# Attention and mixer on one core: the first 768 columns as one block, its second channel product by seven half-size products, and a third raw-score buffer

## The chip, the cores and the metric

The kernel runs on one core of a Trainium2 chip. The metric is the device time of one execution in microseconds (us). In the profile PE is the tensor engine, PEld its weight loads, DVE the vector engine, ACT the scalar engine, POOL the GpSimd engine and SP the engine that issues most DMAs. PEclk is the granted clock of PE, 1.00 being 2.4 GHz.

## The reference

```python
def _attn_ref(q, k, v, w_pre, w_post):            # (4, 12, 448, 64) each; w: 12 x 12
    scores = scale * np.matmul(q, k.transpose(0, 1, 3, 2))
    scores = np.einsum('bhij,hg->bgij', scores, w_pre)
    scores = scores - np.max(scores, axis=-1, keepdims=True)
    attn = np.exp(scores)
    attn = attn / (np.sum(attn, axis=-1, keepdims=True) + 1e-09)
    attn = np.einsum('bhij,hg->bgij', attn, w_post)
    return np.matmul(attn, v)

def _moe_ref(x, w_tok1, w_tok2, w_ch1, w_ch2):    # x: (4, 448, 768)
    h = np.maximum(x.transpose(0, 2, 1) @ w_tok1, 0.0) @ w_tok2
    u = x + h.transpose(0, 2, 1)
    h2 = np.maximum(u @ w_ch1, 0.0) @ w_ch2       # 768 -> 1536 -> 768
    return u + h2
```

The weights of the mixer arrive as float64 and are used as float32. The channel part, `u @ w_ch1`, relu, `@ w_ch2`, is what the change touches most.

## The kernel before

The program is written as Python loops, and each engine executes its instructions in the order in which the loops emit them. Attention fills the first 310 us or so. It goes over groups of rows: PE multiplies q and k into PSUM (`qk`, L152), ACT copies the scores to an SBUF tile `s` (L158), DMAs turn `s` into `r` by rows of heads (L166), and PE mixes heads (`pre`, L174). There are two `s` buffers. Token mixing runs to about 383 us and leaves u = x + h in DRAM (`u_dr`), with the 768 features on partitions in 6 chunks (`KD`) and the 4 x 448 = 1792 columns side by side. It also leaves the split first columns of u in SBUF.

Channel mixing runs from 383 us to the end. A float32 product is made of three matmuls (`mm3`, L708 to L710): each operand is split into a high part (a rounded copy by ACT) and a low part (the operand less its high part, by DVE or POOL), and high x high, high x low and low x high are added up in PSUM.

The columns are done in three blocks. `CB` holds the blocks of 512 and 256 columns; they are done directly. For each of the 12 chunks c of the 1536 hidden features, `ch1(g, c)` multiplies 6 chunks of w1 by the 6 chunks of u (18 matmuls into `pc`), `relu_split` makes high and low part (L704, L705), and `ch2(g, c)` multiplies w2 by them into six accumulators `po` (18 matmuls). After the last c DVE adds u (L850) and SP stores the rows. `split` (ACT L469, DVE L470) makes the high and low part of one chunk of one weight matrix, 768 elements a partition; it runs 48 times, 24 for each block, with six slots. Two of the 48 low parts are on POOL. Behind these blocks, `SB0` = 768, stand the last 1024 columns, done by the Strassen-Winograd scheme: both channel products are divided into 2 x 2 blocks and take seven block products (p = 1, 5, 6, 3, 7, 2, 4) each. That is 28 `stages` of 27 matmuls of 512 columns into `psx` or `psz`. For a stage, `sum_w` (L883) and `sum_x` (L891) make the operands' sums in place on DVE, `split_s` makes high parts (ACT, L901) and low parts (DVE, L903; 1152 elements for the weights, 1536 for x), `mm_s` multiplies, and `evict` copies or adds the result from PSUM (L932 to L958). In the loop over n, the sums and splits for stage n + 2 are emitted ahead of the matmuls of stage n; slots for splits are three. Some results of the second product go to DRAM by an accumulating DMA that POOL issues (L956), and from there to the output.

The float64 weights are read as pairs of 32-bit words and turned to float32 by `wide_tick` (DVE, four instructions, L443 to L453, after an absolute value by ACT); 17 of the 24 chunks are done so during the first block, from loads of 768 KB (`cw_r`, L419). `us`, the 3 MB of u for the last 1024 columns, is loaded by one DMA at 466 us (L988), near the end of the first block.

`WT[w, t]` are the float32 weights in SBUF (w = 0 for w1, 1 for w2; three chunks c in each). `rr` holds the relu of the first product.

Of the kernel before, what the change touches and what calls it, by code (L numbers as in the profile page):

```python
# [33 lines left out]
CB = [(0, 512), (512, 256)]  # L34
SB0 = 768
# [4 lines left out]
def attn_mixer_kernel(  # L40
# [19 lines left out]
    u_dr = dram.tile([128, KD, B * S], F32, name="u_dr")  # L60
    MAG_MIN = 3.0517578125e-05
# [80 lines left out]
    def qk(T, h, home="w", dve=False):  # L142
        b, t = divmod(T, 4)
        n = IT[t][1]
        if T not in S_t:
            S_t[T] = early.tile([120, H, S], F32, tag="s", name="s")
# [263 lines left out]
    CW = [(c, w) for c in range(NC) for w in range(2)]  # L410
# [48 lines left out]
    def split(eng):  # L459
        n = split_at[0]  # L460
        split_at[0] += 1
        c, w = divmod(n % (2 * NC), 2)
        while n < NW and cv_pos[0] <= min(4 * c + 2 * w + 5, len(units) - 1):
            cv_tick(1)
# [3 lines left out]
        hi, lo = [y[:, :768] for y in wslot(n % 6)]  # L468
# [4 lines left out]
    def wslot(i):  # L473
        p = prep["wr"] if i < 3 else prep["wx"]
        return [p.tile([128, 1152 if i < 3 else 768], F32R, tag=f"w{y}{i}", name=f"w{y}") for y in "hl"]
# [255 lines left out]
    def tok2(b):  # L731
# [3 lines left out]
        for d in range(KD):  # L735
# [11 lines left out]
            nc.sync.dma_start(out=u_dr[:, d, S * b:S * b + S], in_=u)  # L747
            if b + 1 < B and d < 4:
                tr(b + 1, (d // 2,), range(2 * (d % 2), 2 * (d % 2) + 2))
# [17 lines left out]
    def u_hi(g, d):  # L767
        if (g, d // 3) not in U:
            U[g, d // 3] = [y.rearrange("p (d n) -> p d n", d=3) for y in xslot(d // 3)]
        return U[g, d // 3][0][:, d % 3, :]  # L770

    def u_lo(g, d, u, c0, c1):
        hi, lo = [y[:, d % 3, c0:c1] for y in U[g, d // 3]]
        nc.gpsimd.tensor_tensor(out=lo, in0=u[:, :c1 - c0], in1=f32(hi), op=ALU.subtract)
# [15 lines left out]
    for w, t in ((0, 0), (1, 0), (0, 1)):  # L790
# [12 lines left out]
    for w, t in ((1, 1), (0, 2), (1, 2), (0, 3), (1, 3)):  # L803
        WT[w, t] = wb.tile([128, 3, 768], F32, name=f"wt{w}{t}")
    wide_open()
    prep["wx"] = en("wx", bufs=1)
    ob = en("ob", bufs=2)
    psb = en("psb", bufs=1, space=PSUM)
    UR, RL, OP = {}, {}, {}
# [10 lines left out]
    def load_u(g):  # L820
        i0, n = CB[g]
        u = urp.tile([128, KD, n], F32, tag=f"ur{g}", name="ur")
        nc.sync.dma_start(out=u, in_=u_dr[:, :, i0:i0 + n])
        UR[g] = u

    def u_k(g, d):
        n = CB[g][1]
        return [y[:, d % 3, :] for y in U[g, d // 3]] if g == 0 else [y[:, n * d:n * d + n] for y in U[g]]

    def ch1(g, c):  # L830
        n = CB[g][1]
        p = psb.tile([128, 512], F32, tag="c1", bufs=2, name="pc1")
        ws = SP.pop(2 * NC * g + 2 * c)
        for d in range(KD):
            mm3(p[:, :n], [w[:, 128 * d:128 * d + 128] for w in ws], u_k(g, d), d == 0, d == KD - 1)
        h = ob.tile([128, 512], F32R, tag="rh", name="rh")
        l = ob.tile([128, 512], F32R, tag="rl", name="rl")
        relu_split(p[:, :n], h[:, :n], l[:, :n])
        RL[g, c] = (h[:, :n], l[:, :n])

    def ch2(g, c, ds=range(KD)):
        i0, n = CB[g]
        ws = SP[2 * NC * g + 2 * c + 1]
        for d in ds:
            if c == 0:
                OP[g, d] = psb.tile([128, 512], F32, tag=f"o{d}", name=f"po{d}")
            mm3(OP[g, d][:, :n], [w[:, 128 * d:128 * d + 128] for w in ws], RL[g, c], c == 0, c == NC - 1)
            if c == NC - 1:
                o = UR[g][:, d, :n]
                nc.vector.tensor_tensor(out=o, in0=OP.pop((g, d))[:, :n], in1=o, op=ALU.add)  # L850
# [209 lines left out]
```

## Time and profile before

| | |
|---|---|
| median of 3 runs | 712.05 us (710.35 to 714.75) |
| the profiled execution | 711.04 us, span 709.2 us, mean granted clock 0.998 |
| busy, share of the span | PE 98%, PEld 69%, DVE 79%, ACT 56%, POOL 34% |
| chain that ended last | PE 94%, DVE 2% |

The profile is one execution. The span runs from its first instruction to its last; the profiled execution's own time is 1.84 us longer. The share of busy time of an engine is an average over stages with different limits.

### The profile page before, as it was taken

To read this page: it belongs to the slowest core of one execution; us is meant where nothing else is said; L and a number is where in the kernel's file an instruction comes from. 1 tells how busy PE (TensorE), PEld (TensorE's weight loads), DVE (VectorE), ACT (ScalarE), POOL (GpSimd) and SP (SyncE) were. 2 spreads that over 40 slices of the span, in tenths; PEclk is the share of its full clock that TensorE was granted. 3 is DMA by queue.
4 is the path that set the end of the run, shared out by engine and by line. 5 is a ranking of instruction groups with operands and counts; after the bars stand their busy time and mean duration, and the time that the engine had idled before them with its cause. 6 is when DMAs were issued, how large, how long until landed. Compare 5 with 4: busy or idle time off the path is not lost.

```text
span 709.2 us, 18841 instructions
## 1 busy us (share of the span) xinstructions
PE 697.5 (98%) x7688; PEld 487.6 (69%) x7688; DVE 563.2 (79%) x835; ACT 397.5 (56%) x743; POOL 240.8 (34%) x222
## 2 busy tenths in 40 slices
PE   8999999999999999999999999999999999999997
PEld 4234544445444444479998888889998888888886
DVE  4777787777777888968898999866778798798982
ACT  3677666766766776545453444343546666755540
POOL 4455666656665776757451000010000000000111
PEclk9999999999999999999999999999999999999999
DMA  6778678658865854665665755272001000000086
GB/s 172 244 224 238 219 218 239 219 171 236 236 216 187 232 172 163 232 198 175 211 220 193 250 168 192 90 266 91 1 6 41 0 1 0 1 1 1 8 172 134
DMA packets 70471, 107.04 MB, mean 151 GB/s; under 512 B 22979, under 2 KB 59376, under 8 KB 70384
## 3 DMA queue, kind: packets, MB, share of 16 engines
q1 hardware_dynamic: 67792, 100.80, 44.8%
q0 software_dynamic: 1680, 3.97, 2.9%
q8 instruction: 61, 1.00, 0.6%
q10 hardware_dynamic: 912, 1.07, 0.6%
q14 instruction: 26, 0.21, 0.1%
HBM read 50.76 MB, written 18.87 MB: 98 GB/s over the span
## 4 chain that ended last, share of the span: by engine, by line
PE 94%; DVE 2%; DMA 1%; issue 1%; POOL 1%; ACT 1%; SPq 0%; POOLq 0%; ACTq 0%; DVEq 0%
PE pre L174 10%; PE post L214 10%; PE av L243 9%; PE qk L152 9%; PE psx L708 5%; PE psx L709 5%; PE psx L710 5%; PE po L709 4%; PE pc L709 4%; PE pc L708 4%; PE pc L710 4%; PE po L710 3%; PE po L708 3%; PE psz L709 3%; PE psz L708 3%; PE psz L710 3%
## 5 line engine op out<-in xcount | busy, mean ns | idle before, releaser
L205 POOL TENSOR_TENSOR e<-e,sm 128x896 f32<-128x896 f32 x90 | 149.5, 1680 | 73.8 <-DVE sm L203 47.0
L158 ACT COPY s<-qk 120x896 f32<-120x896 f32 (+1 forms) x90 | 80.8, 905 | 77.3 <-PE qk L152 68.4
L191 ACT ACTIVATE e<-pre,sm 128x448 f32<-128x448 f32 x180 | 111.8, 635 | 13.5 <-DVE sm L182 7.5
L228 DVE STREAM_TRANSPOSE at<-post 128x896 f32<-128x896 f32 (+1 forms) x98 | 99.4, 1026 | 20.1 <-PE post L214 19.8
L182 DVE TENSOR_REDUCE sm<-pre 128x2 f32<-128x896 f32 x90 | 94.6, 1076 | 8.2 <-PE pre L174 8.2
L174 PE MATMUL pre<-r,kpre 64*64 64x448 f32 (+1 forms) x720 | 89.6, 553 | 1.5 <-ACT e L191 0.9
L152 PE MATMUL qk<-k,q 64*64 64x448 f32 (+2 forms) x768 | 88.9, 540 | 1.9 <-DMA k<-in_k_dram 0.9
L243 PEld LDWEIGHTS av<-at,v 64*64 64x64 f32 x2688 | 71.2, 132 | 22.2 <-ACT s L158 11.6
L214 PE MATMUL post<-e,kpost 64*32 64x448 f32 x1440 | 81.2, 551 | 0.1
L956 POOL DMA_DIRECT2D u_dr<-us x9 | 7.9, 1066 | 207.2 <-DVE us L951 200.8
L243 PE MATMUL av<-at,v 64*64 64x120 f32 (+1 forms) x2688 | 76.0, 258 | 1.8 <-issue 1.3
L174 PEld LDWEIGHTS pre<-r,kpre 64*64 64x64 f32 (+1 forms) x720 | 23.7, 132 | 58.0 <-ACT e L191 31.6
L152 PEld LDWEIGHTS qk<-k,q 64*64 64x64 f32 (+2 forms) x768 | 27.5, 128 | 48.3 <-DVE sm L200 23.4
L469 ACT CAST wh<-wt 128x768 fp32r<-128x768 f32 x48 | 39.7, 832 | 31.7 <-PE po L709 16.6
L708 PE MATMUL psx<-uh,wh 128*128 128x512 f32 x144 | 56.0, 389 | 0.0
L709 PE MATMUL psx<-ul,wh 128*128 128x512 f32 x144 | 56.0, 389 | 0.0
L710 PE MATMUL psx<-uh,wl 128*128 128x512 f32 x144 | 56.0, 389 | 0.0
L901 ACT CAST wh<-wt 128x1152 fp32r<-128x1152 f32 x28 | 32.4, 1158 | 38.5 <-DVE wt L883 27.9
L470 DVE TENSOR_TENSOR wl<-wt,wh 128x768 fp32r<-128x768 f32 x46 | 43.6, 954 | 11.5 <-ACT wh L469 11.5
L903 DVE TENSOR_TENSOR wl<-wt,wh 128x1152 fp32r<-128x1152 f32 x28 | 37.9, 1355 | 17.3 <-ACT wh L901 16.9
L709 PE MATMUL po<-rl,wh 128*128 128x512 f32 (+1 forms) x144 | 48.5, 337 | 0.1
L708 PE MATMUL po<-rh,wh 128*128 128x512 f32 (+1 forms) x144 | 48.4, 336 | 0.0
(123 smaller groups left out, 1431.2 us busy)
## 6 DMA issues: line engine op xcount, KB each, us to landing
r<-s SPq DMA_DIRECT2D x172, 210.0 KB
cw_r<-in_w_ch_dram SPq DMA_DIRECT2D x15, 768.0 KB
xr<-x_dr SPq DMA_DIRECT2D x8, 672.0 KB
cv_r<-in_w_ch_dram SPq DMA_DIRECT2D x14, 384.0 KB
k<-in_k_dram SPq DMA_DIRECT2D x20, 224.0 KB
x_dr<-x SPq DMA_DIRECT2D x36, 120.0 KB
u_dr<-u SPq DMA_DIRECT2D x18, 224.0 KB
q<-in_q_dram SPq DMA_DIRECT2D x22, 180.0 KB
```

What stands on the lines that cost most here:

```text
L152: nc.tensor.matmul(out=p[c:c + m, s, :S], lhsT=Q[T][r, h, c:c + m], rhs=K[b][r, h, :], start=True, stop=True)
L158: nc.scalar.copy(out=S_t[T][:n, h::HP, :], in_=p[:n, :, :S])
L174: nc.tensor.matmul(out=p[64 * s:64 * s + 64, x, :S], lhsT=kpre[k], rhs=rt[a % NR][k], start=True, stop=True)
L182: nc.vector.tensor_reduce(out=s[:m, 0:2], in_=PP[st[0]][:m, :, :S], axis=AX.X, op=ALU.max, negate=True)
L191: nc.scalar.activation(out=E[st[0]][:m, x, :], in_=p[:m, x, :S], func=ACTF.Exp, bias=s[:m, x:x + 1], scale=1.0, accum_out=s[:m, 2 + 2 * x: ...
L205: nc.gpsimd.tensor_tensor(out=e[:m], in0=e[:m], in1=w.to_broadcast([m, 2, S]), op=ALU.mult)
L214: nc.tensor.matmul(out=p[32 * a:32 * a + 32, s, :S].rearrange("p (x g r) -> p x g r", x=2, r=32), lhsT=kpost[k, 32 * hf:32 * hf + 32], rhs ...
L228: nc.vector.transpose(out=AT[T][:, c:c + s1 - s0, :], in_=p[:, s0:s1, :S],)
L243: nc.tensor.matmul(out=p[64 * s:64 * s + 64, u, :10 * w], lhsT=V[b][k, h, j // 2 + JT * (j % 2), :], rhs=at_[k, :w, :, 32 * j + 5 * h:32 * ...
L708: nc.tensor.matmul(out=p, lhsT=a[0], rhs=x[0], start=first, stop=False, skip_group_check=on)
L709: nc.tensor.matmul(out=p, lhsT=a[0], rhs=x[1], start=False, stop=False, skip_group_check=on)
L710: nc.tensor.matmul(out=p, lhsT=a[1], rhs=x[0], start=False, stop=last, skip_group_check=on)
```

## The change

The first 768 columns become one block in both products.

- *First product.* `ch1(c, part, ds)` does 512 columns (part 0) and 256 (part 1) with the same split of w1, so w1 is split once for both: 12 splits instead of 24, in three slots. ACT writes the relu of both parts to `ry`, in float32, with no split. For c = 0 and 1 part 1 is done later (`LAG`), since the u of its columns is loaded by a new DMA on POOL, from a DRAM tile `u1_dr` that token mixing fills with six stores more, and is split behind c = 0. The last c is done in three pieces with the first stages' x splits in between.
- *Second product.* 14 stages stand ahead of the 28: seven products of half size, each in two halves h, 27 matmuls of 384 columns each. Their weights' sums go to new tiles `T`, because `WT` is needed again by the 28 stages. Low parts of the weights are made on POOL in these 14 stages and in four of the last 14 (p = 1 and 5). Low parts of x and all sums stay on DVE. In these stages, and in the last 14, the sums of stage n + 3 are emitted ahead of the low parts of stage n + 2 (`between`). Results are collected in `OA` and added to `u_dr` by 12 accumulating DMAs on POOL, from where SP copies them to the output.
- *Order.* All of w1 is converted before w2 (`CW`). One tick behind each even c, two behind each odd one. The load of `us` is emitted at the ninth stage, when the tiles `T` are free, and `rr` takes the memory of `ry` and of two `OA` tiles.
- *Raw scores.* The tile `s` of attention gets three buffers.

```diff
 CB = [(0, 512), (512, 256)]
+HA = 384
...
-            S_t[T] = early.tile([120, H, S], F32, tag="s", name="s")
+            S_t[T] = early.tile([120, H, S], F32, tag="s", bufs=3, name="s")
...
-    CW = [(c, w) for c in range(NC) for w in range(2)]
+    CW = [(c, w) for w in range(2) for c in range(NC)]
...
-        hi, lo = [y[:, :768] for y in wslot(n % 6)]
+        hi, lo = [y[:, :768] for y in wslot(n % 3)]
...
+            if b == 1:
+                nc.sync.dma_start(out=u1_dr[:, d, :], in_=u[:, CB[1][0] - S:SB0 - S])
...
+    ur = ry[0][:, 1:3, :].rearrange("p a (d n) -> p (a d) n", n=n1)
+    nc.gpsimd.dma_start(out=ur, in_=u1_dr)
...
+    def ch1(c, part, ds):
+        i0, n = CB[part]
+        if 0 in ds:
+            YP[c, part] = pss.tile([128, 512], F32, tag=("a0", "a1", "a2", "b0", "b1", "b2")[2 * (c % 3) + part], name="py")
+        p = YP[c, part][:, :n]
         for d in ds:
+            mm3(p, [w[:, 128 * d:128 * d + 128] for w in SP[c]], [y[:, d % 2, i0:i0 + n] for y in U[d // 2]],
+                d == 0, d == KD - 1)
+
+    def relu(c, part):
+        i0, n = CB[part]
+        nc.scalar.activation(out=ry[c // 3][:, c % 3, i0:i0 + n], in_=YP.pop((c, part))[:, :n], func=ACTF.Relu)
...
-    stages = [(0, g, p, 0) for g in range(2) for p in ORDER] + [(1, 0, p, h) for p in ORDER for h in range(2)]
+    two = [(p, h) for p in ORDER for h in range(2)]
+    stages = [(0, 1, 0, p, h) for p, h in two]
+    NA = len(stages)
+    stages += [(1, 0, g, p, 0) for g in range(2) for p in ORDER] + [(1, 1, 0, p, h) for p, h in two]
...
+        if not blk and p in (5, 6, 3, 7):
+            w = T[h]
...
-            parts.append((*to[n], sources(n)["wx".index(y) + 2]))
-        for hi, lo, src in parts:
+            src = sources(n)["wx".index(y) + 2]
+            parts.append((*to[n], src, nc.gpsimd if y == "w" and (not blk or L and p in (1, 5)) else nc.vector))
+        for hi, lo, src, _ in parts:
             nc.scalar.copy(out=hi, in_=src)
-        for hi, lo, src in parts:
-            nc.vector.tensor_tensor(out=lo, in0=src, in1=f32(hi), op=ALU.subtract)
+        if between is not None:
+            sums(between)
+        for hi, lo, src, eng in parts:
+            eng.tensor_tensor(out=lo, in0=src, in1=f32(hi), op=ALU.subtract)
...
+            if blk:
+                o = (rr if L == 0 else us)[:, d, HN * j:HN * j + HN]
+            else:
+                o = OA[(1, 1) if p == 4 else (i, j)][:, m, :]
...
+            if L == 1 and (p in (3, 7, 2) or p == 4 and not blk):
+                u = u_dr[:, d, i0 + hn * j:i0 + hn * j + hn]
+                nc.gpsimd.dma_start(out=u, in_=o, accum_op=ALU.add)
...
+        while split_at[0] < min(NC, (c if c < LAG else c + 1) + 3):
+            split(nc.vector)
+        for _ in range(1 + (c % 2)):
             wide_tick()
+        if c == NC - 3:
+            split_s(0, "w")
...
     for n in range(len(stages)):
+        if n == 8:
+            close("tp")
+            usp = en("us", bufs=1, side="right")
+            us = usp.tile([128, KD, 2 * HN], F32, name="us")
+            nc.sync.dma_start(out=us, in_=u_dr[:, :, SB0:])
...
-        if 2 < n + 2 < len(stages):
-            sum_w(n + 2)
-            sum_x(n + 2)
-            split_s(n + 2)
+        if 2 <= n + 2 < len(stages):
+            sums(n + 2)
+            split_s(n + 2, between=n + 3 if stages[n + 2][1] else None)
+            if n < NA:
+                sums(n + 3)
         mm_s(n)
         evict(n)
```

The order of instructions, at two places. First POOL, from its last work for token mixing to its end, before: `cv_g` is a step of a weight conversion, `cw_r` the load of float64 weights, `wl` the low part of a weight.

```order
L774 TENSOR_TENSOR ul<-u,uh 128x64 x2
L495 TENSOR_SCALAR cv_g<-cv_g 128x384 x7
L419 DMA cw_r<-in_w_ch_dram 128x1536 x2
L470 TENSOR_TENSOR wl<-wt_4778,wh 128x768 x2
L956 DMA u_dr<-us 128x512 x9
```

After, behind that load and the low parts of the first seven stages: from the eighth stage on (`t` are the tiles of sums, `wt` the weights themselves, `oa` the tiles of results, row by row of 384 columns):

```order
L906 TENSOR_TENSOR wl<-t_6258,wh 128x1152
L906 TENSOR_TENSOR wl<-t_6257,wh 128x1152
L906 TENSOR_TENSOR wl<-t_6258,wh 128x1152
L971 DMA u_dr<-oa 128x384 x3
L906 TENSOR_TENSOR wl<-wt_5615,wh 128x1152
L906 TENSOR_TENSOR wl<-wt_5616,wh 128x1152
L971 DMA u_dr<-oa_6316 128x384 x3
L906 TENSOR_TENSOR wl<-wt_5615,wh 128x1152
L906 TENSOR_TENSOR wl<-wt_5616,wh 128x1152
L971 DMA u_dr<-oa_6315 128x384 x3
```

Two low parts of a direct block gave way to one low part for each of the 14 stages, with three accumulating DMA issues at a time among them.

Second DVE, around the first seven-product stages, before: `pc` and `rl` belong to the first product and the relu of the 256-column block, `ul` is the low part of x.

```order
L470 TENSOR_TENSOR wl<-wt_5606,wh 128x768
L470 TENSOR_TENSOR wl<-wt_5607,wh 128x768
L883 TENSOR_TENSOR wt_5604<-wt_5604 128x3x384
L705 SCALAR_TENSOR_TENSOR rl<-pc_6775,rh 128x256
L470 TENSOR_TENSOR wl<-wt_5606,wh 128x768
L470 TENSOR_TENSOR wl<-wt_5607,wh 128x768
L903 TENSOR_TENSOR ul<-us,uh 128x1536
L705 SCALAR_TENSOR_TENSOR rl<-pc_6828,rh 128x256
```

After, from the end of the last tick (L455) on: L882 is a sum of weights, L890 a sum of x, L906 a low part of x.

```order
L455 SCALAR_TENSOR_TENSOR wt_5616<-cw_r,wt_5616 128x768
L906 TENSOR_TENSOR ul<-ry_5620,uh 128x1152
L906 TENSOR_TENSOR ul<-ry_5621,uh 128x1152
L882 TENSOR_TENSOR t_6257<-wt_5613,wt_5615 128x1152
L890 TENSOR_TENSOR ry_5620<-ry_5620 128x3x384
L882 TENSOR_TENSOR t_6258<-wt_5614,wt_5616 128x1152
L890 TENSOR_TENSOR ry_5621<-ry_5621 128x3x384
L906 TENSOR_TENSOR ul<-ry_5620,uh 128x1152
L882 TENSOR_TENSOR t_6257<-t_6257,wt_5613 128x1152
L890 TENSOR_TENSOR ry_5620<-ry_5622,ry_5620 128x3x384
L906 TENSOR_TENSOR ul<-ry_5621,uh 128x1152
L882 TENSOR_TENSOR t_6258<-t_6258,wt_5614 128x1152
```

Behind the last tick DVE's queue now holds sums and low parts of x for the 14 stages, and no low part of a weight, which POOL has.

## Rows read from the trace of the kernel before

**Rows 1.** The page: busy us, share of the span, instructions.

```profile
PE 697.5 (98%) x7688; PEld 487.6 (69%) x7688; DVE 563.2 (79%) x835; ACT 397.5 (56%) x743; POOL 240.8 (34%) x222
```

**Rows 2.** Windows: stretch, length, busy us of PE, PEld, DVE, ACT, POOL, PEclk, DMA.

```profile
383.00:534.00 151.00, 150.93 (x870) 133.77 (x869) 121.98 (x154) 68.40 (x92) 3.70 (x2) 1.00 0.41 145
534.00:680.00 146.00, 146.00 (x646) 120.93 (x645) 126.45 (x102) 88.03 (x98) 2.71 (x3) 1.00 0.06 12
```

**Rows 3.** Timeline of PE: start, duration (us), engine, line, operation.

```profile
368.26 0.34 PE L708 MATMUL pt<-xn,t 128*128 128x384 f32 x1
...
375.91 0.37 PE L708 MATMUL pt<-t,h 128*128 128x448 f32 x1
...
383.31 0.39 PE L708 MATMUL pc<-uh,wh 128*128 128x512 f32 x1
...
481.25 0.28 PE L708 MATMUL pc<-uh,wh 128*128 128x256 f32 x1
...
533.44 0.40 PE L708 MATMUL psx<-uh,wh 128*128 128x512 f32 x1
```

**Rows 4.** Lines by form: out<-in, shapes, count, busy us, mean ns, idle before.

```profile
L903 DVE TENSOR_TENSOR ul<-rr,uh 128x1536 fp32r<-128x1536 f32 x18 | 31.6, 1758 | 3.7 <-ACT uh L901 3.4
...
L774 POOL TENSOR_TENSOR ul<-u,uh 128x448 fp32r<-128x448 f32 x6 | 6.9, 1151 | 3.7 <-ACT uh L753 3.7
...
L470 POOL TENSOR_TENSOR wl<-wt,wh 128x768 fp32r<-128x768 f32 x2 | 3.7, 1848 | 94.7 <-ACT wh L469 94.7
...
L469 ACT CAST wh<-wt 128x768 fp32r<-128x768 f32 x48 | 39.7, 832 | 31.7 <-PE po L709 16.6 <-DVE wt L453 15.2
```

**Rows 5.** Timeline of DVE: one conversion tick, from 405.75 to the next split.

```profile
405.75 0.55 DVE L443 TENSOR_SCALAR cw_g<-cw_g 128x768 f32<-128x768 f32 x1
...
408.80 0.95 DVE L470 TENSOR_TENSOR wl<-wt,wh 128x768 fp32r<-128x768 f32 x1
```

**Rows 6.** Timeline of DVE in the seven-product stages.

```profile
631.79 1.76 DVE L903 TENSOR_TENSOR ul<-rr,uh 128x1536 fp32r<-128x1536 f32 x1 [0.34 <-ACT uh L901]
633.47 1.35 DVE L883 TENSOR_TENSOR wt<-wt 128x1152 f32<-128x1152 f32 x1
634.74 1.75 DVE L891 TENSOR_TENSOR rr<-rr 128x1536 f32<-128x1536 f32 x1
```

**Rows 7.** Timelines of POOL and DVE where both run; L517's shortest, median, longest ns.

```profile
469.91 1.85 POOL L470 TENSOR_TENSOR wl<-wt,wh 128x768 fp32r<-128x768 f32 x1 [88.44 <-ACT wh L469]
...
471.23 2.14 DVE L970 TENSOR_TENSOR ul<-ur,uh 128x1536 fp32r<-128x1536 f32 x1 [2.02 <-ACT uh L969]
...
322.09 0.77 POOL L521 TENSOR_TENSOR t<-cv_a,t 128x224 fp32r<-128x224 f32 x1 [0.18 <-ACT t L504]
...
322.36 0.92 DVE L517 SCALAR_TENSOR_TENSOR wt<-cv_r,cv_g 128x384 uint32<-128x384 uint32 x1
...
L517 DVE SCALAR_TENSOR_TENSOR wt<-cv_r,cv_g x14: 557/559/916, 322.4 to 379.1; 128x384 uint32<-128x384 uint32 x14
...
354.44 2.95 POOL L495 TENSOR_SCALAR cv_g<-cv_g 128x384 f32<-128x384 f32 x2
...
354.84 0.96 DVE L470 TENSOR_TENSOR wl<-wt,wh 128x768 fp32r<-128x768 f32 x1 [1.05 <-ACT wh L469]
```

**Rows 8.** Timeline of POOL: accumulating DMA issues, the first of three groups.

```profile
671.11 2.71 POOL L956 DMA_DIRECT2D u_dr<-us  x3 [191.20 <-DVE us L951]
```

**Rows 9.** Waits of ACT in attention: us in total, times, longest.

```profile
ACT s L158 <- DMA r<-s: 3.5, 2, 1.9
```

**Rows 10.** Windows during the load of us (DMA share and GB/s at the end).

```profile
471.00:476.00 5.00, 5.00 (x23) 4.14 (x23) 3.79 (x3) 1.52 (x3) 0.76 (x1) 1.00 0.95 387
```

**Rows 11.** Windows around the clock's fall, and one with a lighter gap.

```profile
22.00:23.00 1.00, 0.55 (x8) 0.00 (x0) 0.00 (x0) 1.00 (x4) 0.82 (x1) 1.00 0.98 304
...
24.00:25.00 1.00, 1.00 (x15) 0.15 (x16) 0.50 (x2) 0.48 (x1) 1.00 (x1) 0.50 0.64 224
...
39.00:40.00 1.00, 0.88 (x12) 0.20 (x8) 0.90 (x4) 0.36 (x1) 1.00 (x1) 1.00 0.80 243
```

## What I expect of the change, and why

> **What bounds the kernel now.** I read the page first: PE is busy 697.5 of 709.2 us [rows 1], so time is lost or won where matmuls are added, removed or made to wait. The windows by stage [rows 2] show the stretch that the change touches. While the first 768 columns are done (383 to 534 us) PE is busy 150.93 of 151 us, in the seven-product stages behind them (534 to 680) all of 146, at a granted clock of 1.00. DVE is second there, with 122 and 126 us; POOL is almost unused (3.7 and 2.7). The timeline of PE gives the pace of a matmul by its width [rows 3]. The first 512-column one of the channel products starts at 383.31 and the first 256-column one at 481.25: 97.94 us for 432, 0.2267 us each. From there to the first psx at 533.44 another 432 take 52.19 us, 0.1208 each. In the token product 44 matmuls of 384 columns go from 368.26 to 375.91: 0.1739 each.
>
> **The change, part by part.** *PE work.* Before, the first 768 columns cost 97.94 + 52.19 = 150.13 us. After, their first channel product is still done directly: 12 c of 18 matmuls at 512 and 18 at 256 columns, 216 x (0.2267 + 0.1208) = 75.1 us, 6.25 per c. The second is 14 half-size stages of 27 matmuls at 384 columns, 378 x 0.1739 = 65.7 us, 4.70 a stage. The sum is 140.8, so PE has **9.4 us less** to do. The 28 stages of the other 1024 columns, token mixing and attention keep their matmuls. This is the whole gain that the channel part offers, and it is had only if every operand is there in time.
>
> *DVE, ACT and loads in the first product.* The weights' conversion stays at 17 ticks; one takes DVE 3.05 us, from 405.75 to 408.80 [rows 5]. Two c bring 3 ticks and 2 splits, 9.2 + 2 x 0.95 = 11.1 us on DVE in 12.5; before, two weight matrices were split for each c and the relu's low part came on top. So PE needn't wait here. ACT writes the relu straight to SBUF instead of a split. The conversion loads 17 x 768 KB in some 70 us, 190 GB/s, where 387 GB/s are seen while us is loaded [rows 10]. The load of us itself, 3 MB, now starts at the ninth stage and has five stages (23 us) for about 8 us at that rate. I cost both at nothing; without that cover the us load would cost its 8 us once.
>
> *Third raw-score buffer.* ACT's write of a score tile waits 3.5 us in all, in two places, for the DMA that reads the tile [rows 9]. PE idles little in attention and has work queued ahead in most places. I take −0.3 (0 to −1).
>
> *The 14 new stages.* Here work is added beside PE. Each stage needs a low part of the weights (1152 elements a partition) on POOL and a low part of x (1152) on DVE. Four of the seven products need a sum of w and three, by stage ten, one of x, also on DVE: 8 and 6 for the first ten stages. The order shows the x low parts and the sums alternating on DVE, and on POOL one weights' low part after another, then groups of three accumulating DMA issues. A DVE form of 1152 takes 1.35 us and, back to back, the next starts 1.27 us later (633.47 to 634.74 [rows 6]). POOL has no row of 1152: from 448 elements (1.151) to 768 (1.848) it rises 2.18 ns an element [rows 4], which gives an estimate of 2.69 us. If both engines run side by side they fit: POOL 2.7 and DVE at most 3 x 1.27 = 3.8 in a stage of 4.70.
>
> But the rows speak against side by side. Where a DVE instruction with two SBUF inputs starts while a POOL TENSOR_TENSOR runs, it ends as though it had begun about 0.15 us before POOL's end [rows 7]. POOL ends at 469.91 + 1.85 = 471.76; DVE starts at 471.23 and takes 2.14 where its form takes 1.758 [rows 4], so it ends at 473.37, 1.758 after 471.61. POOL ends at 322.86; DVE's L517 ends at 323.28, its usual 0.557 to 0.559 after 322.72. Against it stands a DVE subtraction at 354.84 beside POOL's TENSOR_SCALAR, not slowed (0.96). The new splits are TENSOR_TENSOR, the operation of the first two, so I count that POOL's low part and DVE's two-input work exclude each other, POOL's for 2.69 − 0.15 = 2.54 us each. The Trainium skill, page "SBUF — State Buffer", section "Who interferes with whom", states such a rule: a DVE instruction with two SBUF inputs contends with a GpSimd one that reads SBUF, and the one that issues second fully blocks. Two of these rows agree with it, the TENSOR_SCALAR row doesn't. By the rule the sum is the one below; by the TENSOR_SCALAR row it is that of the first rival.
>
> With that, let t run from the first matmul of channel product 1. The last split of w1 reuses the slot of c = 8, free at 9 x 6.25 = 56.3; its high copy (0.83 [rows 4]) and low part (0.95) end at 58.1. From there until stage 9, the tenth, can start, DVE and POOL must serve one after the other: four ticks (12.2), ten x low parts and 14 sums (24 x 1.27 = 30.5) and ten weights' low parts (25.4), together 68.1 us, so t = 126.2. Without waits stage 9 would start at 75.1 + 9 x 4.70 = 117.4. **Loss 8.8 us.** Stage 10's weights' low part stands behind three accumulating DMA issues on POOL (2.71 us [rows 8]), 0.8 more than its lead. DVE also waits for ACT's high copies (0.34 at 631.79 [rows 6]), while POOL may have nothing to do either: 1 us in all. Together **+10.6**. Bounds: 6, if the one-input steps of the ticks (4 x 1.1 us of 3.05) run beside POOL; 12, if each of some 30 hand-overs costs a further 0.05. After stage 10 two x sums are left, and a stage with neither sum takes the pair 3.8 us. PE can't catch up, since it is itself the bound afterwards. In the last 14 stages POOL takes four more low parts; in the two of them with sums the pair serves 2.54 + 1.27 + 2 x 1.68 = 7.2 us (1.68 from 631.79 to 633.47 [rows 6]) and PE takes 27 x 0.2267 = 6.1. The two before have no sums (4.2 us), which leaves a lead: 0, at worst 2.
>
> *Sum.* The profiled execution took 711.04 us (span 709.2 and 1.84 around it), 1.0 under the median of the three runs, 712.05. 711.04 − 9.4 − 0.3 + 10.6 = 711.9.
>
> **The rivals.**
> 1. *No exclusion*: POOL's low parts run beside DVE at full speed, as the subtraction at 354.84 did. Nothing in the new stages waits: 711.04 − 9.7 = 701.3. For it: that row, and 2.7 + 3.8 us that fit on two engines. Against: the two TENSOR_TENSOR rows. 0.20. An exclusion for a part of each instruction, or with the ticks' steps let through, gives 705 to 709: 0.17.
> 2. *The clock falls in the new gaps* (slower). With 10.6 us of waiting over ten stages PE is busy some 80%, in holes of 0.4 to 3 us. The trace shows the granted clock at 0.50 (1.2 GHz) at 24 us, after windows in which PE was busy 0.55 of the time, and at 1.00 (2.4 GHz) in a window with 0.88 [rows 11]. At 0.50 a stage takes 9.4 us instead of the 6.4 in which DVE and POOL serve it (3 x 1.27 + 2.54): +3.0 per stage at that level. It decides from three such stages on: 711.9 + 9 = 721. The busy share is nearer to the 0.88 row: 0.08.
> 3. *Late landings*: the accumulating DMAs come back late, and ACT's first copy into the memory that they free waits, or the us load does. By my walk of the order the first has 2.5 us of lead; 5 us late gives 714.4. It is inside the likeliest case's range; 0.02 for more than 719.
>
> **How the numbers follow.** The likeliest case (exclusion, 709 to 716) has 0.53, partial exclusion (705 to 709) 0.17, no exclusion (701 to 704.9) 0.20, the clock or late landings 0.10, of which 0.09 above 719. A change of 1% (7.1 us) is about what a measurement of this kernel can tell from no change. Faster by over 1%, under 704.9: 0.20. Slower by over 1%, above 719.2: 0.09. Within: 0.71. Predicted 711.9 us. The range for 8 in 10 goes from 701.0, just under the no-exclusion sum, since waits that I haven't seen can only lengthen it, to 716.5, and leaves out the clock's case.
>
> **What the profile after would show.** If the steps hold: a first product of about 75 us without idle time on PE; 378 matmuls of 384 columns at 0.174 us; in the 14 stages idle time of PE of 9 to 12 us in all, ended by POOL's or DVE's low parts; low parts and sums on DVE well above 1.35 us in the mean there (2 to 3), POOL's at 2.7 each with little between them, and stages with three DVE instructions of some 6.4 us. If there is no exclusion, DVE's forms keep 1.35 us and the stages 4.70. If the clock falls, the windows there show PEclk under 1.00. If landings are late, ACT waits on a DMA at the first copies of the last 28 stages. The prediction is wrong as a whole if POOL's 1152-element form is not near 2.7 us.

## The result and the profile after

The changed kernel takes 720.99 us (median; 717.9 to 721.54), before beside it 711.58: a ratio of 1.0122, with a 95% interval of 1.009 to 1.0154. It is 1.2% slower. Ratios in this document are taken over the fast runs of both kernels, and can differ by some tenths of a per cent from the quotient of the two medians (1.0132 here). The forecast was 711.9 us with a range of 701.0 to 716.5, so the time lies above the range.

The profiled execution of after took 720.89 us with a span of 719.0. On the page PE is busy 3.1 us less than in [rows 1] (fewer matmuls, but some of them slower, see below), and yet the span is 9.8 us longer. In the chain that ended last DVE has 21%, where it had 2%:

```profile
PE 694.4 (97%) x7634; PEld 491.2 (68%) x7634; DVE 595.4 (83%) x802; ACT 406.1 (56%) x749; POOL 308.9 (43%) x251
...
PE 69%; DVE 21%; ACT 4%; issue 3%; DMA 1%; POOL 1%; SPq 0%; ACTq 0%; DVEq 0%; POOLq 0%
```

The windows of after (columns as in [rows 2]) show where. The first product (380 to 456) and the first of the later stages (541 to 619) run without idle time at a clock of 1.00. In the 14 new stages (456 to 541) PE is idle 12.1 of 85 us, and the granted clock falls to 0.96 and 0.91. POOL, almost unused there before, is busy 49 us.

```profile
380.00:456.00 76.00, 76.00 (x437) 67.20 (x436) 65.84 (x82) 37.74 (x56) 6.33 (x2) 1.00 0.54 191
456.00:502.00 46.00, 40.55 (x217) 38.68 (x216) 45.97 (x24) 21.10 (x26) 26.43 (x7) 0.96 0.00 1
502.00:541.00 39.00, 32.38 (x167) 31.10 (x166) 38.31 (x24) 16.93 (x16) 22.55 (x15) 0.91 0.72 172
541.00:619.00 78.00, 78.00 (x345) 64.57 (x345) 66.86 (x54) 52.66 (x63) 2.69 (x4) 1.00 0.09 16
619.00:648.00 29.00, 26.72 (x118) 21.75 (x118) 27.86 (x15) 16.31 (x19) 12.81 (x4) 1.00 0.00 1
```

The waits of PE from 380 us on (us in total, times, longest) name one releaser, the low part of x on DVE:

```profile
PE psx L710 <- DVE ul L906: 8.9, 4, 4.9
PE psz L710 <- DVE ul L906: 5.3, 4, 2.3
```

And the lines by form show why DVE was late. The same operation on 1152 elements takes 1.348 us where POOL is idle (`wt<-wt`, all but the first from 541 us on) and 2.3 to 3.8 us in the mean of two of its forms in the new stages (`ul<-ry`, `t<-wt`); POOL's own take 3.4 to 3.8 in the mean.

```profile
L906 DVE TENSOR_TENSOR ul<-ry,uh 128x1152 fp32r<-128x1152 f32 x14 | 32.0, 2294 | 0.0
...
L882 DVE TENSOR_TENSOR wt<-wt 128x1152 f32<-128x1152 f32 x6 | 8.1, 1348 | 0.0
...
L882 DVE TENSOR_TENSOR t<-wt 128x1152 f32<-128x1152 f32 x2 | 7.6, 3822 | 0.0
...
L906 POOL TENSOR_TENSOR wl<-wt,wh 128x1152 fp32r<-128x1152 f32 x10 | 31.9, 3389 | 152.3 <-ACT wh L902 83.8 <-DVE cw_g L449 68.5
L906 POOL TENSOR_TENSOR wl<-t,wh 128x1152 fp32r<-128x1152 f32 x8 | 30.2, 3782 | 21.9 <-ACT wh L902 21.9
```

From the starts of consecutive matmuls in PE's timeline the loss can be split: a spacing more than 0.32 us over the pace of its width counts as a wait, what is left over as slow pace: a lower clock, restarts and holes below 0.32. (All times in us. "First" is the start of the first channel product in that profile, "length" from there to the start of the last matmul.)

| kernel | first | length | waits, 14 new stages | slow pace there | waits, last 28 | slow pace there |
|---|---|---|---|---|---|---|
| before | 383.3 | 321.3 | | | 0 | 0 |
| after | 381.0 | 333.6 | 13.0 | 6.0 | 2.4 | 0.2 |
| first 14 on DVE | 379.8 | 324.0 | 1.0 | 0.4 | 7.8 | 2.8 |
| last 4 of the 14 on DVE | 382.1 | 338.7 | 14.7 | 1.3 | 8.0 | 2.7 |
| DMA issues later | 383.2 | 334.3 | 12.8 | 3.1 | 3.7 | 2.8 |
| last 14 on DVE | 381.2 | 330.5 | 13.9 | 4.6 | 0 | 0 |
| all on DVE | 380.6 | 316.6 | 1.0 | 0.4 | 1.6 | 1.7 |
| all on DVE, us in pieces | 380.6 | 312.4 | 0 | 0.4 | 0 | 0 |

(A wait at the change from the 14 to the 28 stages can fall into either column.) For after, 321.3 − 9.4 + 13.0 + 6.0 + 2.4 + 0.2 = 333.5 of the 333.6 measured. The 9.4 us that the fewer matmuls save are there; 21.6 us are lost.

Two places show the mechanism in its two forms, as timelines of POOL, DVE and PE. Some 18 us into the new stages DVE and POOL take turns:

```profile
473.79 3.81 POOL L906 TENSOR_TENSOR wl<-t,wh 128x1152 fp32r<-128x1152 f32 x1 [3.75 <-ACT wh L902]
...
473.71 1.34 DVE L906 TENSOR_TENSOR ul<-ry,uh 128x1152 fp32r<-128x1152 f32 x1
474.98 3.83 DVE L882 TENSOR_TENSOR t<-t,wt 128x1152 f32<-128x1152 f32 x1
478.74 1.34 DVE L890 TENSOR_TENSOR ry<-ry,ry 128x1152 f32<-128x1152 f32 x1
```

POOL's low part is issued at 473.79, while DVE's `ul` of 473.71 runs, and takes 3.81 us instead of 2.67 (its duration at 618.67 us in the same profile, begun with no two-input work on DVE): it waits until DVE's ends, at 475.05, and 1.14 us of that wait show in its duration. DVE's next, at 474.98, waits for POOL in turn: 3.83 instead of 1.35, and ends 1.2 us after POOL. The one behind it runs alone, 1.34. This is the exclusion of [rows 7], with the price put on it: 2.5 us. At the end of the new stages it is worse:

```profile
513.42 1.16 ACT L902 CAST wh<-wt 128x1152 fp32r<-128x1152 f32 x1 [2.46 <-PE psx L710]
...
519.80 2.64 POOL L971 DMA_DIRECT2D u_dr<-oa  x3 [3.26 <-DVE oa L966]
521.50 6.17 POOL L906 TENSOR_TENSOR wl<-wt,wh 128x1152 fp32r<-128x1152 f32 x2
...
521.62 8.54 DVE L906 TENSOR_TENSOR ul<-ry,uh 128x1152 fp32r<-128x1152 f32 x2
...
523.73 0.34 PE L709 MATMUL psx<-uh,wh 128*128 128x384 f32 x1
528.95 0.69 PE L710 MATMUL psx<-ul,wh 128*128 128x384 f32 x1 [4.88 <-DVE ul L906]
```

The first of POOL's two low parts had its high part at 514.58 (513.42 + 1.16). It had to wait until two were due: POOL was busy until 516.54, then stood 3.26 us before the three DMA issues, which are ahead of the low part in its order and need a result of DVE, and the issues took another 1.70 (519.80 to 521.50). The two low parts then go one right behind the other (6.17 us for two), and DVE's `ul` at 521.62 gets in only behind both. The first of its two takes 7.27 us of the 8.54. PE has begun stage 12 at 523.73 and waits 4.88 us for it.

That two low parts are due is not enough for this. At 486.37 two stood next to each other as well, the second with its high part ready at 488.89 (ACT, 487.73 + 1.16), and DVE got its turn between them:

```profile
486.37 7.56 POOL L906 TENSOR_TENSOR wl<-t,wh 128x1152 fp32r<-128x1152 f32 x2 [2.48 <-ACT wh L902]
...
487.56 3.84 DVE L906 TENSOR_TENSOR ul<-ry,uh 128x1152 fp32r<-128x1152 f32 x1
491.33 3.82 DVE L882 TENSOR_TENSOR t<-wt 128x1152 f32<-128x1152 f32 x1
```

In the profiles of after and of the experiments below, the seven pairs of low parts that kept a DVE instruction out for both (7.3 to 8.0 us for it) stand right behind three DMA issues; the pairs in the new stages with no issue right ahead of them never did. Why is open.

### The profile page after: what moved, and what is told of

The parts are those of the page before. It is cut to its first block, busy times and chain, and to the rows that moved or that the text cites. A ratio compares the mean times of both kernels' runs of the same rounds, so it can differ in the third digit from the quotient of the medians.

```text
span 719.0 us, 18762 instructions
## 1 busy us (share of the span) xinstructions
PE 694.4 (97%) x7634; PEld 491.2 (68%) x7634; DVE 595.4 (83%) x802; ACT 406.1 (56%) x749; POOL 308.9 (43%) x251
## 4 chain that ended last, share of the span: by engine, by line
PE 69%; DVE 21%; ACT 4%; issue 3%; DMA 1%; POOL 1%; SPq 0%; ACTq 0%; DVEq 0%; POOLq 0%
PE pre L176 11%; PE post L216 10%; PE qk L154 10%; PE av L245 9%; DVE ul L906 6%; PE psx L710 3%; PE psx L711 3%; PE psx L709 3%; DVE ry L890 3%; PE py L710 2%; PE py L709 2%; PE py L711 2%; PE psz L710 2%; PE psz L711 2%; PE pt L709 2%
## 5 line engine op out<-in xcount | busy, mean ns | idle before, releaser
L193 ACT ACTIVATE e<-pre,sm 128x448 f32<-128x448 f32 x180 | 111.8, 635 | 13.9 <-DVE sm L184 7.5
L906 POOL TENSOR_TENSOR wl<-wt,wh 128x1152 fp32r<-128x1152 f32 x10 | 31.9, 3389 | 152.3 <-ACT wh L902 83.8
L710 PE MATMUL psx<-ul,wh 128*128 128x512 f32 (+1 forms) x216 | 82.5, 382 | 8.9 <-DVE ul L906 8.9
L711 PE MATMUL psx<-uh,wl 128*128 128x512 f32 (+1 forms) x216 | 82.0, 380 | 0.0
L709 PE MATMUL psx<-uh,wh 128*128 128x512 f32 (+1 forms) x216 | 81.7, 378 | 0.0
L710 PE MATMUL psz<-ul,wh 128*128 128x512 f32 (+1 forms) x162 | 60.7, 375 | 5.3 <-DVE ul L906 5.3
L902 ACT CAST wh<-wt 128x1152 fp32r<-128x1152 f32 x34 | 39.4, 1158 | 45.3 <-PE psx L710 15.4
L711 PE MATMUL psz<-uh,wl 128*128 128x512 f32 (+1 forms) x162 | 60.2, 372 | 0.1
L709 PE MATMUL psz<-uh,wh 128*128 128x512 f32 (+1 forms) x162 | 60.1, 371 | 0.0
L710 PEld LDWEIGHTS psx<-ul,wh 128*128 128x128 f32 x216 | 41.9, 194 | 16.0 <-DVE ul L906 10.4
L710 PE MATMUL py<-ul,wh 128*128 128x512 f32 (+1 forms) x144 | 48.5, 337 | 0.0
```

What stands on the lines that cost most here:

```text
L193: nc.scalar.activation(out=E[st[0]][:m, x, :], in_=p[:m, x, :S], func=ACTF.Exp, bias=s[:m, x:x + 1], scale=1.0, accum_out=s[:m, 2 + 2 * x: ...
L709: nc.tensor.matmul(out=p, lhsT=a[0], rhs=x[0], start=first, stop=False, skip_group_check=on)
L710: nc.tensor.matmul(out=p, lhsT=a[0], rhs=x[1], start=False, stop=False, skip_group_check=on)
L711: nc.tensor.matmul(out=p, lhsT=a[1], rhs=x[0], start=False, stop=last, skip_group_check=on)
```

## The experiments

**Low parts of the first 14 stages on DVE.**

```diff
-... nc.gpsimd if y == "w" and (not blk or L and p in (1, 5)) else nc.vector ...
+... nc.gpsimd if y == "w" and (blk and L and p in (1, 5)) else nc.vector ...
```

> The kernel after, with the low parts of the weights of the 14 half-size stages on DVE instead of POOL; nothing else changes. Theory (POOL's TENSOR_TENSOR and DVE's two-input work exclude each other, and the holes lower PE's clock): the 14.0 us that PE waits in these stages and the 4.3 us that it runs at half clock both go; DVE alone has 12.2 + 34 x 1.27 = 55.4 us to do up to the tenth stage, ready at t = 113.5 where PE wants it at 117.4. About 702.5 us, DVE's forms of 1152 back at 1.35 us, granted clock 1.00 there. Rival (POOL's part was needed, DVE is the bound without it): DVE's added 14 x 1.27 = 17.8 us stand on the path, 713 us or more, with PE waiting on DVE's weights' low parts.

Measured: 710.68 us beside 711.26 of before, a ratio of 0.9987 (0.9954 to 1.0019). Of the 18 us that were to go against after, 10 went. In the 14 stages the theory holds: waits fall from 13.0 to 1.0 us and the slow pace from 6.0 to 0.4, so POOL's part was not needed. But two other losses grew: 2.6 us of waits at the change to the last 28 stages (1.0 of them in the first waits column of the table), with 1.3 of slow pace in the 14 stages behind it, and 6.2 and 1.5 in the last 14, where POOL still makes four low parts. The rival's number (713 or more) isn't reached, nor its sign, PE waiting on a weights' low part on DVE.

**Only the last four of these low parts on DVE.**

```diff
-... (not blk or L and p in (1, 5)) ...
+... (not blk and p not in (2, 4) or blk and L and p in (1, 5)) ...
```

> The kernel after, with only the last 4 of the 14 low parts of weights on DVE (p = 2 and 4), the first 10 on POOL as before. Theory: the 4.9 us wait in the eleventh to twelfth stage comes from two POOL low parts running back to back, which keep DVE's x low parts out for both; with them on DVE the 6.1 us of waits after the tenth stage go, and the second fall of the clock (2.6 us) with them: about 712 us, with 8 us of waits left in the first ten stages. Rival (that wait is the backlog of ten stages, not the pair of POOL instructions): DVE has four low parts more to do when it is already late, the waits stay at 5 us or grow, 719 us or more.

Measured: 725.7 us (ratio 1.0193, 1.0132 to 1.0255), 0.7% above after, with intervals that still overlap a little. The time is the rival's, the reason is neither's. After the tenth stage PE has no wait for a low part any more, as the theory said (9.5 us are left in the first ten stages). The stages then reach the 28 later ones sooner, and there ACT waits for the load of us:

```profile
ACT uh L902 <- DMA us<-u_dr: 12.0, 1, 12.0
```

PE waits 5.5 us for ACT's copy of us and 1.6 at the next matmul, and in the last 14 stages 6.0 us. In after ACT's first copy of us waited 6.3 us for this load, but was done at 533.06, some 8 us before PE came to that stage at 540.8: the 4.9 us wait and the slow stretch behind it gave the load most of that time.

**No low part on POOL at all.**

```diff
-... nc.gpsimd if y == "w" and (not blk or L and p in (1, 5)) else nc.vector ...
+... nc.vector ...
```

> The kernel after with no low part on POOL at all (also the four of the last 14 stages). Theory: as with the first 14 on DVE, and the 2.4 us wait in the last 14 stages goes too, since DVE there serves 2 x 1.27 + 2 x 1.68 = 5.9 us in a stage of 6.1: about 700 us. Rival (DVE too full in the last 14): the wait stays or grows, 702.5 us or more.

Measured: 703.94 us (ratio 0.9896, 0.9846 to 0.9945). It is faster than before. The wait in the last 14 stages is gone, 6.7 us less than with the first 14 alone, so DVE isn't too full there. What keeps it from 700 is the change to the last 28 stages: 2.6 us of waits and 2 at slow pace. Waits of ACT, then the timelines of SP's queue and of ACT:

```profile
ACT uh L902 <- DMA us<-u_dr: 7.6, 1, 7.6
...
499.88 4.87 SPq L822 DMA_DIRECT2D out_dram<-u_dr  x6
504.92 0.62 SPq L1025 DMA_DIRECT2D us<-u_dr  x1
...
521.26 1.47 ACT L902 CAST uh<-us 128x1536 fp32r<-128x1536 f32 x1 [7.60 <-DMA us<-u_dr]
```

SP issues the load behind six output stores that wait for accumulating DMAs, at 504.92; ACT's first copy of us can start at 521.26, 16.3 us later, while the accumulating DMAs and stores share the DMA engines.

**us in four pieces**, on top of it, in the order in which the stages need them.

```diff
-nc.sync.dma_start(out=us, in_=u_dr[:, :, SB0:])
+for d, c0 in ((0, 0), (0, HN), (3, HN), (3, 0)):
+    nc.sync.dma_start(out=us[:, d:d + 3, c0:c0 + HN], in_=u_dr[:, d:d + 3, SB0 + c0:SB0 + c0 + HN])
```

> All low parts on DVE, and the load of us cut into four DMAs in the order in which the stages need the quarters. Theory: what was left with all low parts on DVE (1.0 + 1.6 us of waits for ACT's copy of us, which itself waits 7.6 us for the load, and 2 us at half clock behind them) goes, since the first quarter of 768 KB lands some 5 us after its issue and not 16: 699.6 us. Rival (the wait is that of a full DVE at the change of stages): within 1 us of the kernel with all low parts on DVE, 703 us or more.

Measured: 699.2 us (ratio 0.9824, 0.98 to 0.9849), as expected. PE has no wait from 380 us to the last matmul; the windows show DVE full but in time (43.97 of 44 us), with PE busy 21.00 of 21 where us is loaded:

```profile
456.00:500.00 44.00, 43.96 (x253) 43.64 (x253) 43.97 (x37) 26.61 (x30) 2.70 (x3) 1.00 0.07 8
500.00:521.00 21.00, 21.00 (x123) 21.00 (x122) 19.79 (x19) 9.89 (x9) 5.23 (x6) 1.00 0.99 257
...
597.00:626.00 29.00, 29.00 (x129) 24.01 (x129) 27.23 (x22) 18.89 (x23) 0.00 (x0) 1.00 0.00 1
```

This version beats both kernels. Its length of 312.4 us is before's 321.3 less 8.9.

**The DMA issues behind the next low part.**

```diff
-                nc.gpsimd.dma_start(out=u, in_=o, accum_op=ALU.add)
-                o_row[0] = d
-                store_out(i0 + hn * j, u)
+                LATER.append((u, o, d, i0 + hn * j))
...
             split_s(n + 2, between=n + 3 if stages[n + 2][1] else None)
+            flush()
```

`flush` issues what is in `LATER`, each with its output store.

> The kernel after, with each group of three accumulating DMA issues of the first 14 stages emitted behind the next weights' low part on POOL instead of ahead of it; all low parts stay on POOL. Theory (the issues delay a low part by 2.7 us, so that two low parts then run back to back and shut DVE out for 6.2 us): the low parts are apart again, the waits after the tenth stage fall from 6.1 to 1 to 2 us and the second fall of the clock goes: 713 to 715 us. Rival (the pairs come from elsewhere, or the backlog): within 1.5 us of the kernel after, 720 us.

Measured: 720.25 us (ratio 1.0118, 1.0064 to 1.0171), not told from after. The waits after the tenth stage fall from 6.1 to 3.6 us (2.6 and 1.0) and the slow pace in the new stages from 6.0 to 3.1, but the last 14 stages lose 6.4 us instead of 2.6. The rival has the time. One pair of POOL's low parts still stands together, and a DVE sum waits behind both, 7.97 us:

```profile
512.67 2.72 POOL L948 DMA_DIRECT2D u_dr<-oa  x3
514.42 6.32 POOL L906 TENSOR_TENSOR wl<-wt,wh 128x1152 fp32r<-128x1152 f32 x2
...
513.99 7.97 DVE L890 TENSOR_TENSOR ry<-ry,ry 128x1152 f32<-128x1152 f32 x1
```

The edit moves the issues by one low part, and the pair again stands right behind three of them. So it parts one pair and not the other, and it neither clears the issues of the loss nor shows that the backlog has a share.

**The last 14 stages on DVE, the first 14 on POOL.**

```diff
-... (not blk or L and p in (1, 5)) ...
+... not blk ...
```

> The kernel after with the four low parts of the last 14 stages on DVE; the first 14 stay on POOL. Theory (each of the two places waits for itself): the 2.4 us wait in the last 14 stages goes, 0 to 3 us for lost clock with it: 716 to 718.5 us. Rival (the two places are one backlog): 720 us or more.

Measured: 717.46 us with before at 713.63 beside it, a ratio of 1.0045 (1.0012 to 1.0079); against after's 1.0122 that is 0.8%, 5.5 us less. The wait and the slow pace there are 0 in the profile. So these four low parts cost some us by themselves: 2.6 in the profile of after, 5.5 between these runs, 6.7 between the two kernels with the first 14 on DVE.

**POOL only writes.**

```diff
-eng.tensor_tensor(out=lo, in0=src, in1=f32(hi), op=ALU.subtract)
+if eng is nc.gpsimd:
+    eng.memset(f32(lo), 0.0)
+else:
+    eng.tensor_tensor(out=lo, in0=src, in1=f32(hi), op=ALU.subtract)
```

> The kernel after, but POOL writes zeros where it makes a low part (18 of them), so that it reads nothing; the products miss these parts. Theory (the lock is on reading SBUF): DVE's forms of 1152 keep 1.35 us beside POOL's, PE's waits in the 14 stages fall from 13 to 2 us or less: 700 to 706 us. Rival (any POOL instruction keeps DVE out): DVE's forms are longer by POOL's duration, and the waits stay, 715 us or more if a fill takes 2 us or more.

Measured in one execution: 699.64 us. DVE's sums take 1.352 us in the new stages; POOL makes 18 fills of 1.18:

```profile
L882 DVE TENSOR_TENSOR t<-wt 128x1152 f32<-128x1152 f32 x2 | 2.7, 1352 | 0.0
...
L882 DVE TENSOR_TENSOR wt<-wt 128x1152 f32<-128x1152 f32 x2 | 2.7, 1352 | 0.0
...
L907 POOL MEMSET wl<- 128x1152 f32 x18 | 21.2, 1176 | 185.6 <-PE psx L711 93.4 <-PE py L711 75.2 <-PE psz L711 17.1
```

PE doesn't wait at all in the new stages. A fill is shorter than a low part and needs no high part, so the time alone would not settle it. The overlaps do: a two-input DVE instruction of 1152 elements that runs beside a fill takes 1.35 or 1.36 us, in the whole profile, as here:

```profile
456.60 1.06 POOL L907 MEMSET wl<- 128x1152 f32 x1 [5.24 <-PE py L711]
...
457.00 1.35 DVE L882 TENSOR_TENSOR t<-wt,wt 128x1152 f32<-128x1152 f32 x1
```

So it is not POOL's being busy that holds DVE: an instruction that reads nothing doesn't.

**POOL reads one input.**

```diff
-eng.tensor_tensor(out=lo, in0=src, in1=f32(hi), op=ALU.subtract)
+if eng is nc.gpsimd:
+    eng.tensor_scalar(out=lo, in0=src, scalar1=0.5, scalar2=2.0, op0=ALU.mult, op1=ALU.mult)
+else:
+    eng.tensor_tensor(out=lo, in0=src, in1=f32(hi), op=ALU.subtract)
```

> The kernel after, but POOL makes each of the 18 low parts by a TENSOR_SCALAR of the weights alone (one input, no subtraction), so the products are not what they should be. The nearest rows of before, 384 elements in 1.54 us and 224 in 0.99, give some 4.1 us for 1152. Theory (as the row at 354.84 had it, POOL's TENSOR_SCALAR doesn't keep DVE out): DVE's forms stay at 1.35 us, waits of a few us at most where POOL itself is late: 703 to 710 us. Rival (any POOL instruction that reads SBUF keeps DVE's two-input ones out): with 4 us instead of 2.5 shut out per stage it is slower than the kernel after, 735 us or more.

Measured in one execution: 701.58 us. The time is the theory's, its reason is wrong. The instruction was far shorter than estimated, 1.16 us where DVE left it alone (at 444.67), and it does hold DVE out:

```profile
459.26 2.13 POOL L907 TENSOR_SCALAR wl<-t 128x1152 fp32r<-128x1152 f32 x1 [6.95 <-DVE t L882]
...
459.02 1.35 DVE L890 TENSOR_TENSOR ry<-ry 128x1152 f32<-128x1152 f32 x1
460.29 2.30 DVE L882 TENSOR_TENSOR t<-wt,wt 128x1152 f32<-128x1152 f32 x1
```

POOL's of 459.26 waits for the end of DVE's at 460.37 and runs to 461.39; DVE's of 460.29 takes 0.95 us longer than 1.35 and ends 1.2 us behind POOL. Only the price is small, 1 us a stage, and it fits in the 4.70. So the row at 354.84 of [rows 7], beside which I had set a case of its own, doesn't speak for TENSOR_SCALAR in general. It was no single case either: the other DVE subtraction of that form that ran inside such a clamp of before, at 372.54 us, took 0.95 us. Why DVE was not held there (a clamp with max and min, 1.48 us for 384 elements) stays open.

**The third raw-score buffer alone, and taken away.** Three kernels: before with it, the best version without it, and after without it.

```diff
-S_t[T] = early.tile([120, H, S], F32, tag="s", name="s")
+S_t[T] = early.tile([120, H, S], F32, tag="s", bufs=3, name="s")
```

> The kernel before with the third raw-score buffer alone. Theory (the waits for the DMA that reads a tile were covered by queued work): 0 to 1 us less than before, 710.5 us. Rival (the 2.3 us by which the first product starts earlier in the profile of after come from this buffer): 709 us, and a first product that starts before 381.5 us in its profile.

> All low parts on DVE, us in four pieces, and the raw scores back in two buffers: the channel part alone against before. Theory (PE's 9.4 us less and nothing else in the channel part; the buffer alone gave 4.2 us): 711.5 - 8.5 to 9.4 = 702 to 703 us. Rival (the buffer's 4.2 us were a matter of the draw of runs, and the profiles' 1.5 us are the size): 700.5 us or less.

> The kernel after with two raw-score buffers instead of three. Theory (the buffer gives 4 us wherever the rest stands): 721 + 4.2 = 725 us. Rival (its gain lies in the lower clock that before has at 20 to 30 us in its profile, which comes and goes): 721 to 723 us.

Measured: before with the buffer 707.38 us, ratio 0.9936 (0.9913 to 0.9958); the best version without it 706.68 beside 713.63, 0.9883 (0.9831 to 0.9935) where it has 0.9824 with it; after without it 724.57, 1.0139 (1.0088 to 1.0191) where it has 1.0122. The first comparison gives 0.6% (4 us) for the buffer, more than its theory had (0 to 1 us). The second gives 0.6% too and the third 0.2%, both with intervals so wide that they hold 4 us as well as almost nothing. The waits of ACT before a raw-score copy in the profile of before with the buffer:

```profile
ACT s L158 <- PE qk L152: 75.2, 81, 1.9
```

The wait for the DMA of [rows 9] is gone, and so are two others of before that had been put down to a load of v (3.3 us) and to PE (2.1 us); what remains is the wait for PE, 75.2 us where before has 68.4. The first product of the channel part starts at 381.3 us in the mean of the ten profiles with three buffers (379.8 to 383.2), at 384.8 in the three with two (382.9 to 388.0). So the buffer is worth some 4 us by the clearest of the three comparisons, and a single pair of profiles says little of it, since this start varies by more than 3 us between kernels with the same attention code.

## Why the prediction was wrong

*The bound and PE's arithmetic* were right: the length of the best version is 8.9 us under before's, 9.4 was forecast (its own terms, 150.13 − 140.8, give 9.3), and the matmuls of 384 columns kept 0.174 us.

*The mechanism* of the first ten stages was right. POOL's TENSOR_TENSOR and DVE's two-input instructions exclude each other; POOL's 1152 took 2.67 us where 2.69 was estimated, with 2.5 us held against the 2.54 counted, and the fill, which reads nothing, holds nobody. For the first ten stages the sum says 8.8 us of loss; the seven holes there make 2.40 + 1.54 + 0.61 + 0.21 + 0.22 + 1.47 + 1.47 = 7.9. The Trainium skill, page "SBUF — State Buffer", section "Who interferes with whom", has the rule, and its two halves (reading contends, only writing doesn't) agree with the 3.83 and the 1.352 us. POOL's clamp in before, which reads too, does not follow it (the DVE subtractions at 354.84 and 372.54 us). The lower bound of that term was unfounded: a one-input step of the conversion was held as well, 3.04 us where it takes 0.55, beside POOL's of 451.56:

```profile
451.56 2.84 POOL L906 TENSOR_TENSOR wl<-wt,wh 128x1152 fp32r<-128x1152 f32 x1 [0.52 <-ACT wh L902]
...
451.79 3.04 DVE L445 TENSOR_SCALAR cw_g<-cw_g 128x768 f32<-128x768 f32 x1
```

*The step that failed*: three terms of the sum were mis-sized, two of what comes behind the tenth stage, and the clock.

1. "Stage 10's weights' low part stands behind three accumulating DMA issues on POOL (2.71 us [rows 8]), 0.8 more than its lead." I priced the issues alone. They also wait for a result of DVE (3.26 us at 519.80) and hold back what stands behind them, and I had not asked what the delay does to the order of the two engines: POOL's next low part is due as the first ends, the two run together, and DVE is out for 6.2 us with x low parts in its queue that PE needs first. Waits after the tenth stage: 6.1 us (0.28, 0.48, 5.04, 0.31) against 0.8 and the 1 us for hand-overs. With the last four low parts on DVE these waits went. Every pair that shut DVE out stands right behind DMA issues, so they belong to the cause as far as is known; no run has such a pair without them.
2. "The two before have no sums (4.2 us), which leaves a lead: 0, at worst 2." The four low parts of the last 14 stages cost 2.6 us in the profile of after, 5.5 us in the runs.
3. The clock. It was the second rival, at 0.08, and I held holes of this size to be nearer to a window with 0.88 of busy PE, where it stayed at 1.00, so the sum had nothing for it. After two of the long holes the granted clock fell to 0.50 (the 1.2 GHz level). Windows of 2 us, the columns as in [rows 11]:

```profile
456.00:458.00 2.00, 0.49 (x4) 0.23 (x2) 1.97 (x3) 0.63 (x2) 0.00 (x0) 1.00 0.00 0
458.00:460.00 2.00, 1.27 (x6) 1.27 (x7) 2.00 (x3) 0.00 (x0) 0.00 (x0) 0.87 0.00 0
460.00:462.00 2.00, 2.00 (x8) 2.00 (x7) 2.00 (x2) 0.70 (x1) 0.00 (x0) 0.50 0.03 8
...
526.00:528.00 2.00, 0.00 (x0) 0.00 (x0) 2.00 (x1) 0.00 (x0) 1.67 (x1) 0.93 1.08 318
...
530.00:532.00 2.00, 2.00 (x8) 2.00 (x8) 2.00 (x5) 0.41 (x1) 1.07 (x2) 0.50 0.89 222
```

PE stood idle 2.2 us at 456 and 4.9 at 524; the level was 0.50 for 3.4 and 6.8 us (the second began while PE was still idle), 26 matmuls of 384 columns took 0.32 us instead of 0.174 each, and some 4 of the 6 us at slow pace in the table are theirs. Holes of 1.3 us (496, 502) had no fall behind them, and 2.3 us at 638.8 had none in this profile, while 3.1 us at about the same place had one in three others. The first hole of the new stages, 2.2 us in after and 2.2 to 2.4 in three of the experiments with the first low parts on POOL, had no fall in those three and one in a fourth. What decides between them stays open. The rival had whole stages at half the clock, +3.0 us each; what came were two stretches shorter than a stage, which cost some 1.6 and 2.4 us.

The sum had 10.6 us for all that PE loses; the profile has 21.6: 0.9 less than forecast in the holes of the first ten stages, 4.3 more in those of the next four, 2.4 more in the wait of the last 14, and 5.2 at slow pace. *The third buffer* was a term of its own, −0.3 (at best −1); the first product starts 2.3 us earlier in this pair of profiles, and the runs give the buffer some 4. I read it from one row of ACT's waits and took the other waits of the same instruction for other causes, though a wait for several semaphores is put down to the one that came last. 711.9 + 11.0 − 2.0 = 720.9 is the profiled execution's own time.

*Late landings* were costed at nothing with a cover of 23 us. The load of us was issued behind stores, at 517.44 in after, and took 14.1 us to ACT's first copy (11.9 to 19.3 in the other kernels whose ACT waits for it) where I reckoned 8 from a stretch without accumulating DMAs. In after it cost PE nothing, since the pair of low parts held PE longer. It was the next loss as soon as that was mended.

## What to carry to other kernels

Before an elementwise operation is given to a second engine, add up the times of all instructions that exclude each other, and not what each engine is busy. Over the first ten stages that was 24 x 1.27 + 10 x 2.54 = 55.9 us against PE's 47.0, a loss; all on one engine it was 34 x 1.27 = 43.2, a gain. Where two engines exclude each other, ask which of them the bound engine needs first, and whether the other can get two in a row; look at what stands ahead of an instruction in its engine's order, and what that in turn waits for. When PE is left with holes of several us, reckon with a stretch at the lower clock behind them, and look for what the hole was covering: here it hid a load that was the next loss.

## What the runs showed of the hardware that I had not expected

- A one-input DVE TENSOR_SCALAR of 768 float32 elements took 3.04 us beside POOL's TENSOR_TENSOR instead of 0.55.
- POOL's TENSOR_SCALAR (mult, mult) of 1152 elements took 1.16 us, against 1.48 for 384 elements with max and min, and held DVE's two-input instruction for 0.95 us.
- Two POOL TENSOR_TENSOR right behind three DMA issues kept a waiting DVE instruction out for both (7.27 us for one of 1.35). With no issue right ahead of them the two engines mostly took turns one by one, also where POOL's second was due in time (486.37); in two of the experiments three DVE instructions in a row kept POOL's out (6.28 us for one of 2.67, at 463.60 with the last four low parts on DVE).
- The same 3 MB load took 16.3 us to ACT's first copy among accumulating DMAs and stores (all low parts on DVE), and some 10 us in before, where it ran without them.
